# Dynamic convolution and squared-ReLU FFN on one core: convolution steps, closing transposes and group loads moved to other steps of a chunk, the last chunk stored plainly

## Chip, core and metric

The kernel runs on one core of a Trainium2 chip. The metric is the device time of one execution in microseconds; runs of a kernel are summed up by their median. "PE" is TensorE (matrix products; "PEld" its weight loads), "DVE" VectorE, "ACT" ScalarE, "POOL" GpSimd, "SP" SyncE, which here does nothing but issue DMAs, one after another.

## What is computed

First a convolution whose seven weights are made anew for each token and head (a softmax over `weight_gen`), over the seven latest tokens; then an FFN with the square of a ReLU, on 32768 tokens of width 192, hidden width 2048:

```
w   = softmax(weight_gen, axis=-1)                       # 8 x 4096 x 8 heads x 7 taps
out = einsum('bshk,bskhg->bshg', w, the 7 latest x)      # 24 columns per head
h   = out.reshape(32768, 192) @ w_in                     # 192 -> 2048
y   = (maximum(h, 0) ** 2) @ w_out                       # 2048 -> 192
```

## The kernel before, in words

**Chunks and steps.** Token rows are dealt out over 128 partitions, 256 rows each; a chunk is 4 of these rows, 512 tokens, and there are NCH = 64 chunks. A chunk has NJ = 8 steps; a step makes two of the 16 hidden blocks of 128 columns ("fb"). The main loop goes over chunks c = 1 to 63 and in them over steps j = 0 to 7 (written c/j below). All engines work through their instructions in the order in which this loop emits them; the schedule is by hand.

**A step of the main loop** emits, in this order: `mm1(c, j)`, 18 matmuls of 512 columns (line 439), which go in pairs on the upper and the lower 64 rows of the array; `mm2_turned` of two steps earlier (LAG = 2; line 512), 20 such matmuls, which add into four PSUM banks; on ACT two ReLUs (L456) and two squares (L460); on DVE the two `low` parts of the step before (L468), which `mm2_turned` will read a step later; after the last `mm2_turned` of a chunk (at step 1 of the next) `sum_turned`, two ACT copies (L520) and two DVE additions (L522) that free the banks, and a DMA `raw<-raw` (L523); then whatever the dictionary `todo` holds for this step; then `store_turned` in two parts; then on ACT the two `high` parts (L464), from which and from the squares the next step's `low` is made.

**The convolution of chunk m** is a list of 20 steps from `conv_steps`: six of the softmax (0 max, 1 subtract, 2 exp on ACT, 3 sum, 4 reciprocal, 5 multiply; L244 to L249), then thirteen products (L275) and additions (L288), all on DVE over 128x768 elements, then `turn`: a DVE transpose (L402), four DMAs to DRAM (`xd`, L408) and two back (`xT`, L413). Before, `spread` lays these evenly over eight steps from CONV_BEG = 3: (m-2)/3 to (m-1)/2, in numbers 3, 2, 3, 2, 3, 2, 3, 2. At (m-1)/6 three ACT casts (`xh`, L316) and three DVE subtractions (`xl`, L319) split the result, and m/0 reads it.

**Loads and stores.** A group is two chunks. `load_group` issues one DMA of the weights `wt` (L116) and one of `x` (L117), at step 0 of odd chunks, for the group whose convolution begins in the next chunk; it is emitted ahead of everything else of its step. `store_turned(c-1, 0)` at OUT_STEP = 5 is a DVE transpose (L531) and 16 DMAs `o_sb<-raw` (L540); `store_turned(c-1, 1)` at step 6 is a DVE addition that needs `raw<-raw` (L533), a transpose (L534), 8 DMAs and the four of `put_out` to the output (L77). All of them are on SP.

**The last chunk** (63) has its `mm2` the other way round, tokens on the output's partitions (L485, then L774 and L777); its ReLUs, which for odd blocks above 2 are on DVE (L452), also reorder the tokens, so that `put_out` with reads = 1 finds each token by four DMAs, one per 32 partitions. There are three such stores.

Of the kernel before, what the change touches and what calls it, by code (L numbers as in the profile page):

```python
# [21 lines left out]
def kernel(  # L22
# [9 lines left out]
    nc = tc.nc  # L32
# [5 lines left out]
    Q = 32  # L38
    HALO = K - 1
    R = B * S // P  # L40
    PPB = S // R
    TC = 4
    NCH = n_chunks or R // TC
    TG = 8
    CPG = TG // TC
# [4 lines left out]
    NJ = NF // 2  # L50
# [1 line left out]
    WI = ND * P  # L52
    N_PE = 2
    LAG = 2
    CONV_BEG = 3
    OUT_STEP = 5
    NBUF = NF // 2

    const = ctx.enter_context(tc.tile_pool(name="const", bufs=1))
# [12 lines left out]

    def put_out(c, t0, t1, o_sb, reads):
        rows = slice(rows_of(c) + t0, rows_of(c) + t1)
        v = out.rearrange("(q a b r) d -> q b a r d", q=P // Q, a=2 ** reads, r=R)
        for q in range(P // Q):
            nc.sync.dma_start(out=v[q, :, :, rows, :], in_=o_sb[q * Q:(q + 1) * Q, t0:t1])  # L77
# [15 lines left out]
    def rows_of(c):  # L93
        return (c + CPG if c < CPG else c - CPG if c < 2 * CPG else c) * TC
# [8 lines left out]
    def load_group(gi):  # L103
        t0 = rows_of(gi * CPG)
        xt = xin.tile([P, TG + HALO, D], F32, name="xt")
        wt = xin.tile([P, TG, H, K], F32, name="wt")
        x_tiles[gi], w_tiles[gi] = xt, wt
        wf = wt.rearrange("p t h k -> p t (h k)")
        if gi == 0:
            nc.sync.dma_start(out=wf[:, 0:TC, :], in_=wg_v[:, t0:t0 + TC, :])  # L110
            nc.sync.dma_start(out=xt[:, HALO:HALO + TC, :], in_=x_v[:, t0:t0 + TC, :])
            for h in (HALO // 2, 0):
                nc.sync.dma_start(out=xt[:, h:h + HALO // 2, :], in_=x_v[:, t0 - HALO + h:t0 - HALO // 2 + h, :])
            return
        if t0 > 0:
            nc.sync.dma_start(out=wf, in_=wg_v[:, t0:t0 + TG, :])  # L116
            nc.sync.dma_start(out=xt, in_=x_v[:, t0 - HALO:t0 + TG, :])  # L117
            return
        nc.gpsimd.memset(xt[:, 0:HALO, :], 0.0)
        nc.sync.dma_start(out=wf, in_=wg_v[:, 0:TG, :])  # L120
        nc.sync.dma_start(out=xt[:, HALO:, :], in_=x_v[:, 0:TG, :])
        for p0 in range(0, P, PPB):
            nc.sync.dma_start(
                out=xt[p0 + 1:p0 + PPB, 0:HALO, :],
                in_=x_v[p0:p0 + PPB - 1, R - HALO:R, :],
            )
# [97 lines left out]
    def conv_steps(c, on_pe, moving=False):  # L224
# [3 lines left out]
        n = TC * H  # L228
# [28 lines left out]
        prs = {}  # L257
# [139 lines left out]
        def turn():  # L397
            xr = att.tile([P, D // Q, P], F32, name="xr")
            xT = att.tile([P, ND, N], F32, name="xT")
            for k in range(ND):  # L400
                src[k] = xT[:, k]
            nc.vector.transpose(  # L402
                xr.rearrange("p b (t j) -> p t b j", j=Q),
                prs.pop(0).rearrange("p t (b i) -> p t b i", i=Q),
            )
            xd = dram.tile([D, N], F32, name="xd")
            for q in range(P // Q):
                nc.sync.dma_start(  # L408
                    out=xd[:, q * P:(q + 1) * P].rearrange("(b i) n -> i b n", i=Q),
                    in_=xr[q * Q:(q + 1) * Q],  # L410
                )
            for h in range(2):
                nc.sync.dma_start(out=xT[h * D1:(h + 1) * D1], in_=xd.rearrange("(k p) n -> p k n", p=D1))  # L413
# [6 lines left out]
    def mm1(c, j, ops=range(9)):  # L420
        xh, xl = xts[c]["h"], xts[c]["l"]
        if (c, 2 * j) not in phs:
            if c == 0 and j < 2:
                two = [ps_o.tile([P, N], F32, name=f"acc{b + 2 - 2 * j}") for b in range(2)]
            elif c == 0 and j % 2:
                two = [ps_o.tile([P, N], F32, name=f"acc{b}") for b in (2, 3)]
            else:
                two = [ps_h.tile([P, N], F32, name="ph") for _ in range(2)]
            phs[c, 2 * j], phs[c, 2 * j + 1] = two
        two = phs[c, 2 * j], phs[c, 2 * j + 1]  # L430
        seq = [(q, xx, k) for q, xx in ((0, xh), (0, xl), (1, xh)) for k in range(ND)]
        for n, (q, xx, k) in enumerate(seq):
            if n not in ops:
                continue
            for i in range(2):
                rows = slice(i * D1, (i + 1) * D1)
                kw = (k + i) % ND if c < N_PE else k
                w = W[rows, q, j, kw * P:(kw + 1) * P]
                nc.tensor.matmul(two[i], w, two_streams(xx[rows, k]), start=(n == 0), stop=(n == len(seq) - 1))  # L439
# [18 lines left out]
    def square(c, fb):  # L458
        r = rgs[c, fb]
        nc.scalar.activation(r, r, AF.Square)  # L460
# [86 lines left out]
    outs = {}  # L547

    def finish(c, t, to=None):
        if c not in outs:  # L550
            o_sb = op.tile([P, TC, D], F32, name="o_sb", bufs=2)
            outs[c] = o_sb, stage.tile([P, TC, 2 * D], F32, name="raw") if c > 0 else None
        o_sb, tmp = outs[c]
        acc = accs[c][t]
        if c == 0:
            nc.scalar.copy(o_sb[:, 2 * t:2 * t + 2, :], acc[:, 0:2 * D].rearrange("p (t d) -> p t d", t=2))
        else:
            nc.scalar.copy(tmp[:, t, D:], acc[:, D:2 * D])
            to = o_sb[:, t] if to is None else to
            for h, l in ((slice(0, P), slice(2 * P, 2 * D)), (slice(P, D), slice(D, 2 * P))):  # L560
                nc.vector.tensor_tensor(out=to[:, h], in0=acc[:, h], in1=tmp[:, t, l], op=ALU.add)

    def store(c, t0, t1):
        put_out(c, t0, t1, outs[c][0], 1)


    nc.vector.memset(warm, 0.0)
# [115 lines left out]
    def at(c, j, f):  # L683
        todo.setdefault((c + j // NJ, j % NJ), []).append(f)

    def spread(fs, c, j0, j1):
        for i, f in enumerate(fs):
            at(c, j0 + (j1 - j0) * i // len(fs), f)

    def plan_conv(m, a, b):  # L690
        if m == 3:
            for f in a[:2]:
                at(1, 1, f)
            soon[1, 2] = a[2:3]
            spread(a[3:], 1, CONV_BEG, CONV_BEG + NJ)
        elif m > 3:
            spread(a, m - 2, CONV_BEG, CONV_BEG + NJ)
        else:
            for j, fs in enumerate(((), a[4:5], a[5:8], a[8:])):
                for f in fs:  # L700
                    at(1, j, f)
        if m < 2 + CPG:
            soon[m - 1, NJ - 1] = b[0] + b[1][:ND * (m == 2)]
            for f in b[1][ND * (m == 2):]:
                at(m - 1, NJ - 1, f)
        else:
            for f in b:
                at(m - 1, NJ - 2, f)
# [6 lines left out]
    for c in range(1, NCH):  # L715
        tail = c == NCH - 1
        for j in range(NJ):
            if j == 0 and c % 2 and (c + 3) // 2 * CPG < NCH:
                load_group((c + 3) // 2)
            if j == CONV_BEG and 1 < c < NCH - 2:  # L720
                plan_conv(c + 2, *conv_steps(c + 2, 0))
            if c == 1 and j == 0:
                for t in range(TC // 2):
                    finish(0, t)
                store(0, 0, TC)
            mm1(c, j)
            fbs = (2 * j, 2 * j + 1)
            done = None
            if len(pend) == LAG or tail and pend:
                c2, j2 = pend.pop(0)  # L730
                for fb in (2 * j2, 2 * j2 + 1):
                    mm2_turned(c2, fb)
                done = c2 if j2 == NJ - 1 else None
            for f in soon.pop((c, j), []):
                f()
            for fb in fbs:
                relu(c, fb)
            for fb in fbs:
                square(c, fb)
            if not tail:  # L740
                pend.append((c, j))
            for f in late:
                f()
            late.clear()
            if done is not None:
                sum_turned(done)
            for f in todo.pop((c, j), []):
                f()
            if c > 1 and j == OUT_STEP:
                store_turned(c - 1, 0)  # L750
            if c > 1 and j == OUT_STEP + 1:
                store_turned(c - 1, 1)
            if not tail or j < NJ // 2:
                for fb in fbs:
                    high(c, fb)
                    late.append(lambda c=c, fb=fb: low(c, fb))
    c = NCH - 1
# [13 lines left out]
    t, end = TC - 1, range(NF - 4, NF)  # L771
# [6 lines left out]
    o_sb, tmp = outs[c]  # L778
# [33 lines left out]
```

## Time and profile before

| | |
|---|---|
| time, median of 3 runs (lowest to highest) | 2147.02 us (2146.01 to 2150.02) |
| time of the profiled execution | 2143.92 us |
| its span, first to last instruction | 2142.2 us |
| granted TensorE clock, mean | 0.999 (the 2.4 GHz level) |
| busy: PE, PEld, DVE, ACT | 2131.4 (99%), 2044.4 (95%), 1857.5 (87%), 1797.9 (84%) |
| DMA | 195.33 MB, mean 91 GB/s |

The profiled execution is 3.1 us below the median of the timed runs. A share of busy time does not tell whether PE runs at its pace: an instruction that starts late shows as a busy one all the same, so the pace is read from the starts of the matmuls. Times in the rows below count from the start of the span.

### The profile page before, as it was taken

What the parts mean: (1) busy time and instruction counts of PE and PEld (TensorE: products, weight loads), DVE (VectorE), ACT (ScalarE), POOL (GpSimd) and SP (SyncE); (2) the same over time, 40 slices, a digit from 0 to 9 for tenths busy, and PEclk for the clock granted to TensorE, in tenths of its full rate; (3) what the DMA queues carried; (4) which work ended last, traced back from release to release, by engine and by line L of the source; (5) the groups of instructions that cost most, each with busy time, mean ns of one, the idle gap of its engine ahead of it and who ended that gap; (6) DMA issues with size and microseconds to landing.
All of it is one profiled execution on the core that took longest, in us unless ns stands there. A gap on an engine that the chain in (4) does not pass through costs nothing.

```text
span 2142.2 us, 50282 instructions
## 1 busy us (share of the span) xinstructions
PE 2131.4 (99%) x19486; PEld 2044.4 (95%) x19486; DVE 1857.5 (87%) x2866; ACT 1797.9 (84%) x3492; POOL 9.9 (0%) x18
## 2 busy tenths in 40 slices
PE   9999999999999999999999999999999999999998
PEld 9889999999999999999999999999999999999998
DVE  9988988888889888888898888888988888889884
ACT  8888888888888888888888888888888888888886
POOL 0000000000000000000000000000000000000000
PEclk9999999999999999999999999999999999999999
DMA  8433334333233332333433333334333233333231
GB/s 230 100 80 102 88 66 104 88 96 92 62 105 93 91 105 62 93 102 84 103 89 66 104 87 97 91 63 104 91 93 104 62 92 94 91 104 87 67 76 39
DMA packets 324303, 195.33 MB, mean 91 GB/s; under 512 B 225128, under 2 KB 282472, under 8 KB 320224
## 3 DMA queue, kind: packets, MB, share of 16 engines
q1 hardware_dynamic: 322768, 188.58, 34.9%
q0 software_dynamic: 1296, 3.54, 0.9%
q8 instruction: 152, 2.49, 0.5%
q14 instruction: 87, 0.71, 0.1%
HBM read 106.39 MB, written 49.55 MB: 73 GB/s over the span
## 4 chain that ended last, share of the span: by engine, by line
PE 96%; DVE 1%; SPq 1%; ACT 1%; DMA 0%; issue 0%; DVEq 0%; ACTq 0%
PE acc L512 49%; PE ph L439 45%; PE acc L476 1%; PE acc L485 1%; SPq L540 1%; DMA xT<-xd 0%; DVE gl L468 0%; ACT gh L464 0%; ACT rg L460 0%; DMA out_dram<-o_sb 0%; ACT rg L456 0%; DVE du L184 0%; DVE du L186 0%; PE acc L439 0%; DVE xl L319 0%
## 5 line engine op out<-in xcount | busy, mean ns | idle before, releaser
L512 PE MATMUL acc<-gh,V 64*128 64x512 f32 x5952 | 1085.2, 377 | 0.0
L512 PE MATMUL acc<-gl,V 64*128 64x512 f32 x3968 | 917.4, 378 | 0.6 <-DVE gl L468 0.5
L439 PE MATMUL ph<-xh,W 64*128 64x512 f32 x6084 | 917.7, 376 | 0.2
L512 PEld LDWEIGHTS acc<-gh,V 64*128 64x128 f32 x5952 | 779.9, 186 | 25.6
L468 DVE TENSOR_TENSOR gl<-rg,gh 128x512 fp32r<-128x512 f32 x1008 | 641.3, 675 | 119.6 <-ACT gh L464 119.6
L439 PEld LDWEIGHTS ph<-xh,W 64*128 64x128 f32 x6084 | 709.8, 186 | 24.8 <-issue 0.7
L456 ACT ACTIVATE rg<-ph 128x512 f32<-128x512 f32 x992 | 537.8, 594 | 218.1 <-PE ph L439 217.4
L460 ACT ACTIVATE rg<-rg 128x512 f32<-128x512 f32 x1008 | 579.8, 631 | 0.2
L512 PEld LDWEIGHTS acc<-gl,V 64*128 64x128 f32 x3968 | 556.3, 186 | 23.6 <-DVE gl L468 3.3
L464 ACT CAST gh<-rg 128x512 fp32r<-128x512 f32 x1008 | 574.2, 624 | 3.2 <-PE acc L485 3.2
L439 PE MATMUL ph<-xl,W 64*128 64x512 f32 x3042 | 459.3, 376 | 0.0
L275 DVE TENSOR_TENSOR pr<-xt,wt 128x768 f32<-128x768 f32 (+1 forms) x441 | 411.1, 945 | 2.3
L439 PEld LDWEIGHTS ph<-xl,W 64*128 64x128 f32 x3042 | 355.3, 186 | 11.6
L288 DVE TENSOR_TENSOR pr<-pr 128x768 f32<-128x768 f32 x366 | 345.8, 945 | 0.1
L319 DVE TENSOR_TENSOR xl<-xT,xh 128x512 fp32r<-128x512 f32 x186 | 117.5, 687 | 123.0 <-ACT xh L316 120.2
L316 ACT CAST xh<-xT 128x512 fp32r<-128x512 f32 x186 | 102.6, 622 | 1.8 <-DMA xT<-xd 1.7
L246 ACT ACTIVATE wt<-wt 128x224 f32<-128x224 f32 x62 | 24.2, 391 | 94.8 <-DVE wt L245 94.8
L522 DVE TENSOR_TENSOR raw<-acc,raw 128x512 f32<-128x512 f32 x124 | 79.0, 675 | 3.8 <-ACT raw L520 3.8
L520 ACT COPY raw<-acc 128x512 f32<-128x512 f32 x124 | 66.5, 596 | 0.0
L402 DVE STREAM_TRANSPOSE xr<-pr 128x768 f32<-128x768 f32 x62 | 60.7, 978 | 2.1
L534 DVE STREAM_TRANSPOSE raw<-raw 64x512 f32<-64x512 f32 x62 | 43.6, 704 | 2.1
L531 DVE STREAM_TRANSPOSE raw<-raw 128x512 f32<-128x512 f32 x62 | 43.7, 704 | 0.0
(93 smaller groups left out, 450.4 us busy)
## 6 DMA issues: line engine op xcount, KB each, us to landing
xT<-xd SPq DMA_DIRECT2D x124, 384.0 KB
xt<-in_x_dram SPq DMA_DIRECT2D x30, 1344.0 KB
out_dram<-o_sb SPq DMA_DIRECT2D x252, 96.0 KB
xd<-xr SPq DMA_DIRECT2D x248, 96.0 KB
o_sb<-raw SPq DMA_DIRECT2D x1488, 16.0 KB
raw<-raw SPq DMA_DIRECT2D x62, 128.0 KB
wt<-in_weight_gen_dram SPq DMA_DIRECT2D x31, 224.0 KB
raw<-in_moe_w_in_dram SPq DMA_DIRECT2D x16, 192.0 KB
```

Source lines behind the costliest of these rows:

```text
L275: tt(out=dst, in0=src, in1=wf[:, t0 * H:t1 * H, k:k + 1].broadcast_to([P, m, G]), op=ALU.mult)
L288: tt(out=prs[k0], in0=prs[k0], in1=prs.pop(k), op=ALU.add)
L316: nc.scalar.copy(parts["h"][:, k, n], src[k][:, n])
L319: tt(out=parts["l"][:, k, n], in0=src[k][:, n], in1=parts["h"][:, k, n].bitcast(F32), op=ALU.subtract)
L439: nc.tensor.matmul(two[i], w, two_streams(xx[rows, k]), start=(n == 0), stop=(n == len(seq) - 1))
L456: nc.scalar.activation(r, ph, AF.Relu)
L460: nc.scalar.activation(r, r, AF.Square)
L464: nc.scalar.copy(gh, rgs[c, fb])
L468: nc.vector.tensor_tensor(out=gl, in0=rgs.pop((c, fb)), in1=ghs[c, fb].bitcast(F32), op=ALU.subtract)
L512: nc.tensor.matmul(accs[c][b + h], w, two_streams(g[rows]), **fl)
L520: nc.scalar.copy(X[:, k], acc[b])
L522: nc.vector.tensor_tensor(out=X[:, k], in0=acc[b + 1], in1=X[:, k], op=ALU.add)
```

## The change

- The 20 convolution steps of a chunk (from chunk 4 on) begin at step 1 instead of 3 and are dealt out in the numbers 2, 1, 4, 1, 3, 0, 3, 3, 0, 3 over ten steps, (m-2)/1 to (m-1)/2. Chunk 3's keep their steps.
- `store_turned` moves from steps 5 and 6 to steps 3 and 4.
- `load_group` moves from step 0 to step 5 of the odd chunks (not in chunk 1).
- The last chunk's `turn` makes four transposes of 128x192 instead of one of 128x768, and writes them in an order such that the tokens come out plainly; its three stores are one DMA each instead of four.

```diff
-    CONV_BEG = 3
-    OUT_STEP = 5
+    CONV_BEG = 1
+    CONV_SLOTS = (2, 1, 4, 1, 3, 0, 3, 3, 0, 3)
+    OUT_STEP = 3
+    LOAD_STEP = 5
...
         rows = slice(rows_of(c) + t0, rows_of(c) + t1)
+        if reads == 0:
+            nc.sync.dma_start(out=out.rearrange("(p r) d -> p r d", r=R)[:, rows, :], in_=o_sb[:, t0:t1])
+            return
...
-            nc.vector.transpose(
-                xr.rearrange("p b (t j) -> p t b j", j=Q),
-                prs.pop(0).rearrange("p t (b i) -> p t b i", i=Q),
-            )
+            pr = prs.pop(0).rearrange("p t (b i) -> p t b i", i=Q)
+            if c < NCH - 1:
+                nc.vector.transpose(xr.rearrange("p b (t j) -> p t b j", j=Q), pr)
+            else:
+                for t in range(TC):
+                    nc.vector.transpose(xr[:, :, t * Q:(t + 1) * Q].rearrange("p b (i m) -> p b m i", i=2), pr[:, t])
...
     def store(c, t0, t1):
-        put_out(c, t0, t1, outs[c][0], 1)
+        put_out(c, t0, t1, outs[c][0], 1 if c == 0 else 0)
...
-            spread(a[3:], 1, CONV_BEG, CONV_BEG + NJ)
+            spread(a[3:], 1, 3, 3 + NJ)
         elif m > 3:
-            spread(a, m - 2, CONV_BEG, CONV_BEG + NJ)
+            fs = iter(a)
+            for j, n in enumerate(CONV_SLOTS):
+                for _ in range(n):
+                    at(m - 2, CONV_BEG + j, next(fs))
...
-            if j == 0 and c % 2 and (c + 3) // 2 * CPG < NCH:
+            if j == (LOAD_STEP if c > 1 else 0) and c % 2 and (c + 3) // 2 * CPG < NCH:
                 load_group((c + 3) // 2)
             if j == CONV_BEG and 1 < c < NCH - 2:
                 plan_conv(c + 2, *conv_steps(c + 2, 0))
```

## Rows read from the trace of the kernel before

**Rows 1.** The page: the chain that ended last, share of the span by engine.
```profile
PE 96%; DVE 1%; SPq 1%; ACT 1%; DMA 0%; issue 0%; DVEq 0%; ACTq 0%
```
**Rows 2.** Timeline of PE, first matmuls of steps 30/0, 30/1, 31/0: start, length, instruction, count.
```profile
1006.07 0.95 PE L439 MATMUL ph<-xh,W 64*128 64x512 f32 x6
...
1010.31 0.81 PE L439 MATMUL ph<-xh,W 64*128 64x512 f32 x6
...
1039.02 0.94 PE L439 MATMUL ph<-xh,W 64*128 64x512 f32 x6
```
**Rows 3.** Timeline of PE: first matmuls of step 4/0 and of step 63/0.
```profile
149.20 0.38 PE L439 MATMUL ph<-xh,W 64*128 64x512 f32 x2
...
2094.51 0.38 PE L439 MATMUL ph<-xh,W 64*128 64x512 f32 x1
```
**Rows 4.** Timeline of all engines, step 30/0, where its second product begins.
```profile
1007.57 1.24 DVE L468 TENSOR_TENSOR gl<-rg,gh 128x512 fp32r<-128x512 f32 x2
...
1008.02 0.51 PE L512 MATMUL acc<-gh,V 64*128 64x512 f32 x2
...
1008.27 0.48 PE L512 MATMUL acc<-gl,V 64*128 64x512 f32 x2
```
**Rows 5.** Timeline of DVE, steps 29/6 to 30/3; the bracket is idle time and its end.
```profile
1002.67 1.90 DVE L319 TENSOR_TENSOR xl<-xT,xh 128x512 fp32r<-128x512 f32 x3 [2.00 <-ACT xh L316]
1004.48 0.95 DVE L275 TENSOR_TENSOR pr<-xt,wt 128x768 f32<-128x768 f32 x1
...
1006.22 0.68 DVE L533 TENSOR_TENSOR raw<-raw 64x512 f32<-64x512 f32 x1
...
1014.29 1.28 DVE L468 TENSOR_TENSOR gl<-rg,gh 128x512 fp32r<-128x512 f32 x2
1015.49 1.27 DVE L522 TENSOR_TENSOR raw<-acc,raw 128x512 f32<-128x512 f32 x2
...
1021.47 0.98 DVE L402 STREAM_TRANSPOSE xr<-pr 128x768 f32<-128x768 f32 x1
...
1023.55 0.38 DVE L244 TENSOR_REDUCE mx<-wt 128x32 f32<-128x224 f32 x1
```
**Rows 6.** Timeline of ACT, the copies of `sum_turned` at step 30/1.
```profile
1014.46 1.07 ACT L520 COPY raw<-acc 128x512 f32<-128x512 f32 x2
```
**Rows 7.** Timeline of SP's DMA issues, from step 30/4 to 31/3.
```profile
1022.48 2.65 SPq L408 DMA_DIRECT2D xd<-xr  x4
1026.83 1.32 SPq L413 DMA_DIRECT2D xT<-xd  x2
1032.46 16.42 SPq L540 DMA_DIRECT2D o_sb<-raw  x24
1048.99 3.06 SPq L77 DMA_DIRECT2D out_dram<-o_sb  x4
1052.10 0.43 SPq L116 DMA_DIRECT2D wt<-in_weight_gen_dram  x1
```
**Rows 8.** Stretches of a group's load: length, busy time by engine, clock, DMA share, GB/s.
```profile
1052.10:1053.10 1.00, 1.00 (x12) 1.00 (x10) 1.00 (x3) 0.55 (x2) 0.00 (x0) 1.00 0.38 147
1053.10:1054.60 1.50, 1.50 (x17) 1.50 (x15) 1.47 (x3) 1.00 (x3) 0.00 (x0) 1.00 0.98 270
...
1052.10:1058.30 6.20, 6.20 (x61) 6.20 (x59) 5.17 (x10) 3.63 (x9) 0.00 (x0) 1.00 0.87 298
```
**Rows 9.** Tile `wt`, window 1040 to 1090: first and last start of its first reader.
```profile
L244 DVE TENSOR_REDUCE mx<-wt x2: 377/378/378, 1056.5 to 1089.4; 128x32 f32<-128x224 f32 x2
```
**Rows 10.** The last chunk: DVE and SP timelines, and the chain's last piece of `mm1`.
```profile
2111.08 0.69 DVE L452 TENSOR_SCALAR rg<-ph 128x512 f32<-128x512 f32 x1
...
2110.90 4.15 PE ph L439 x36
...
2133.69 0.36 DVE L780 TENSOR_TENSOR o_sb<-ph,raw 128x192 f32<-128x192 f32 x1
...
2128.66 10.99 SPq L77 DMA_DIRECT2D out_dram<-o_sb  x16
```

## The prediction

> **What bounds the kernel now.** I read the chain first: 96% of it is PE [rows 1], so nothing counts that does not delay PE or stand at the two ends. Next PE's pace, from the starts of its matmuls. From step 30/1 to 31/0 seven steps take 1039.02 - 1010.31 = 28.71 us, 4.10 each, but step 30/0 takes 1010.31 - 1006.07 = 4.24 [rows 2]: 0.14 too long, though PE shows as busy throughout. It is no single case: from 4/0 to 63/0 59 chunks take 2094.51 - 149.20 = 1945.3 us, 32.97 each [rows 3], and eight steps at 28.71 / 7 are 32.81. So 0.16 us a chunk, 59 x 0.16 = **9.4 us**, is lost to this wait and a few larger ones.
>
> What does PE wait for in step 30/0? Its second product should start some 0.22 after the first (step 4.10 over 19 pairs), at 1008.24; it starts at 1008.27, with 0.48 for the pair [rows 4], and from there on the two halves of each pair, which had run 0.14 apart, run together (six matmuls take 0.81 in 30/1 and 0.95 in 30/0 [rows 2]): the first half has slipped by that much. It reads the first `gl` of step 29/6, which DVE only begins at 1007.57 and makes in about 0.64. DVE is late because of what 29/6 put ahead of it: three `xl` that had to wait 2.00 us for ACT, then a product, an addition and the second part of `store_turned`, from 1004.48 to 1007.57 [rows 4, 5]. So the loss is DVE's queue at step 6, not DVE's total.
>
> There is a second thing to see: at step 1 `sum_turned` starts on DVE at 1015.49, right behind two `gl` (1014.29) [rows 5], although ACT's first copy is done by about 1015.0 [rows 6]. It ends at 1016.76, and PE wants the banks again at step 2. This is as tight as the other.
>
> **The change part by part.**
>
> *Convolution steps and OUT_STEP.* Nothing is added on DVE; the same work goes to other steps. Prices, start to start [rows 4, 5]: product or addition 0.87 (two from 1004.48 to 1006.22); two `gl` 1.20; three `xl` 1.81; second part of the store 1.35 (1006.22 to 1007.57); the `turn` 0.91 and the store's first transpose 0.65 (both taken just under the duration of such a row); two sums 1.20; small softmax steps 0.4 to 0.6 (`mx` 0.38). DVE per step, `gl` included:
> before, steps 0 to 7: 2.9, 5.0, 3.0, 2.0, 2.2, 4.0, 6.1, 3.8;
> after: 3.8, 3.2, 3.9, 4.1, 3.4, 3.8, 3.0, 3.8.
> Before, step 6 is 2.0 over PE's 4.10 and step 1 0.9; after, no step is over. Now the queue after the change, in chunk 30's times. At 29/6 the `xl` still end at 1004.48, as ACT sets them. The `gl` of 29/6 come directly behind: first one by 1005.1, wanted at 1008.1, so 3.0 early instead of 0.1 late. Three products (2.61) and the next `gl`: 1008.9 against 1012.2, 3.3 early. Three more: 1012.7 against 1016.3, 3.6. `sum_turned` then finds DVE free and follows ACT's copies, 1015.0 to 1016.2, 0.5 sooner than now. Two softmax steps, `gl` at 1017.6 (wanted 1020.4, 2.8 early: the least). Two additions and the `turn` end at 1020.9 (now 1021.47 + 0.91 = 1022.4), `gl` at 1021.5 (3 early), four softmax and product steps and the transpose, `gl` at 1025.6 (3), a product and 1.35, `gl` at 1029.1 (3.7). DVE never owes PE anything; 2.8 us is the cover, and if it goes each us more costs PE one. So all of the 9.4 us should go. ACT's load stays; `exp` moves to step 2, after its input. Ends: 8.0 (59 x 0.137, the larger waits stay) to 9.6.
>
> *SP's queue.* It now reaches `xd` at 1020.9. Rows 7 give 2.65 for its issues, 1.70 until it has landed, 1.32 for `xT`: 1026.6. Y is ready (1025), so 24 `o_sb` in 16.5 and four stores in 3.1 follow without a gap: 1046.2. `xT` is read at about 1034.8 and lands some 4 after issue: early by 4. SP is free for the next chunk's `raw<-raw` at about 1049.
>
> *Loads.* Now they are issued at 1052.10, ahead of the odd chunk's own work, and first read at 1089.4: 37 us ahead [rows 7, 9]. After, they stand behind the odd chunk's stores, at 1046.2 in these times, and the first reader comes at 1016.2 + 32.8 = 1049.0: **2.8 us ahead**. How long does `wt` take? By 1054.60, 2.5 after issue, 147 + 405 = 552 KB had moved [rows 8], more than `wt` (224) and what could be left of three stores (288). Lower end 1.6 (0.43 issue and 224 KB at 298 GB/s), upper end 6.2, if it landed only with all of the group. I take 2.5, the nearest row: just in time. At 6.2 DVE would stand 3.4, of which 2.8 is covered: 0.6 for PE, 29 times, 17 us. `x` lands by 1052.4, its first product comes at 1056. The Trainium skill, DMA: Bandwidth & Descriptors, section Rules for kernel authors, says to issue a DMA early, compute, and wait on it late; this part does the contrary, and by that rule the load becomes a rival (below). No run shows yet which.
>
> *The last chunk.* Its `turn` is four transposes instead of one: 0.98 now; four between 4 x 0.25 (a quarter of the row) and 4 x 0.7. Chunk 62 has no convolution beside it (nothing of a chunk 64), so DVE covers up to 2.8 more; I take 0. Store: the result is ready at 2133.69 + 0.36 = 2134.05, but SP is then in a row of 16 issues from 2128.66 to 2139.65 [rows 10], and the span ends 2.5 after it, at 2142.2. After, SP has chunk 62's stores behind it earlier and only three issues: last one 2134.1 to 2134.7 (10.99 / 16 = 0.69; 0.43 for 128 rows of `wt`), and the end at 2137.2: **5.0 saved**. Ends: 3.5 (a DMA of 128 rows takes as long to land as four) to 5.3. Against it: the store's two parts now precede the DVE ReLU of step 63/5, 2.0 us in all, some of it in idle time; that ReLU ends at about 2113.3 instead of 2111.8, and PE, which does the last 36 matmuls from 2110.90, wants its bank at about 2112.9 [rows 10]. **0.4 lost** (0 to 0.8).
>
> *Start.* Chunk 0 to 2/0 keep their order: nothing.
>
> **Sum.** 9.4 + 5.0 - 0.4 = 14.0 us. The profiled execution would go from 2143.92 to 2129.9. The median of the runs stands 3.1 above it (2147.02); kept, that gives **2133.0 us**.
>
> **The rivals.**
>
> A. *The wait only moves.* PE's matmuls run in pairs; a pair's second half starts 0.14 after its first in some stretches and together with it in others (0.95 for six against 0.81 [rows 2]), so one half can slip without the other, and freeing one wait may uncover another at step 2, as the banks come free late. For it: both waits are as tight. Against it: DVE is 2.8 early everywhere, `sum_turned` by 0.5. Then only the end gains: 2147.0 - 4.6 = 2142.4. Chance 0.10, half of it beyond the bound below.
>
> B. *The load comes late* (slower). The trace gives `wt` 2.8 us and it needs 2.5; DVE covers another 2.8. Beyond 3.1 late PE stands, in each of 29 groups, and the gain is gone at 14.0 / 29 = 0.5 more, so at 6.1 us after issue, or an issue that late. SP has no gap ahead of it, so each stretched issue adds. With 1 us of PE per group: 2133 + 29 = 2162. For it: `xd` and `xT` wait on landings in front of it. Against it: nothing else moves on the queues then. Chance 0.10, a third of it within the bound or faster.
>
> C. *The end gives less*, as the 128-row store lands late or the ReLUs of chunk 63 hold PE longer: 2135 to 2137. Chance 0.08. The forecast itself (2129 to 2136): 0.72.
>
> **How the numbers follow.** A measurement of this kernel can tell about 0.2% (4.3 us) from no change, so the bound is 2142.7. Faster: 0.72 + 0.08 + 0.05 + 0.01 = 0.86; within: 0.05 + 0.02 = 0.07; slower 0.07. The range: the forecast's terms at their ends (8.0 + 3.5 - 0.8 = 10.7 to 9.6 + 5.3 = 14.9) give 2132.1 to 2136.3; timed runs differ by 4 us, and what keeps them above the profiled one may be waits of the same kind, which 2.8 us of cover would also take: down to 2129. Upwards it takes in A, to 2143; of B's end only the part up to there, as the rows put `wt` at 2.5.
>
> **What would show it.** In the profile after: step 30/0 as long as the others, eight steps in 32.81; `gl` of step 6 done 3 us ahead of its product; DVE's first addition of `sum_turned` right after ACT's first copy; `xd` issued some 1.6 earlier in a chunk; SP without a gap from `xT` to the last store; `mx` of an even chunk with an idle time before it that ends with `wt`, or none; three store issues at the end, the last at about 2.5 us before the end of the span. It would be wrong if a step other than 0 is longer than 4.10, or if `mx` of even chunks waits over 2.8 us for `wt`.

## The result and the profile after

The changed kernel takes 2129.07 us in the median (2128.74 to 2129.46), beside 2147.49 (2146.01 to 2150.02) of the kernel before: a ratio of 0.9916, 95% interval 0.9904 to 0.9929, so 18.4 us less. 14.0 were forecast (2133.0 us). The profiled execution went from a span of 2142.2 us to 2126.9, 15.3 less. Line numbers of the changed kernel are 5 to 10 higher: `mm1` is L446, `mm2_turned` L519, `low` L475, `put_out` L78 (plain) and L82.

The chain that ended last, share by engine [rows 1]:

```profile
PE 99%; ACT 0%; POOL 0%; issue 0%; DVE 0%; POOLq 0%
```

PE's timeline: the first matmuls of steps 30/0, 30/1 and 31/0 [rows 2], then those of 4/0 and 63/0 [rows 3] (start, length, instruction, count):

```profile
1001.50 0.81 PE L446 MATMUL ph<-xh,W 64*128 64x512 f32 x6
...
1005.60 0.81 PE L446 MATMUL ph<-xh,W 64*128 64x512 f32 x6
...
1034.31 0.81 PE L446 MATMUL ph<-xh,W 64*128 64x512 f32 x6
```
```profile
148.53 0.38 PE L446 MATMUL ph<-xh,W 64*128 64x512 f32 x2
...
2084.12 0.59 PE L446 MATMUL ph<-xh,W 64*128 64x512 f32 x4
```

Step 30/0 now takes 4.10 like the seven behind it. From 4/0 to 63/0 the 59 chunks take 1935.6 us, 32.81 each, where they took 32.97: 9.7 us less, and nothing is left of the wait (no step of these chunks is longer than 4.10). Six matmuls take 0.81 in all three rows: both halves of a pair now run together through the chunk.

DVE's timeline, steps 29/6 to 30/3 [rows 5] (the bracket is idle time and what ended it):

```profile
998.10 1.90 DVE L324 TENSOR_TENSOR xl<-xT,xh 128x512 fp32r<-128x512 f32 x3 [1.97 <-ACT xh L321]
999.91 1.29 DVE L475 TENSOR_TENSOR gl<-rg,gh 128x512 fp32r<-128x512 f32 x2
...
1010.37 1.29 DVE L529 TENSOR_TENSOR raw<-acc,raw 128x512 f32<-128x512 f32 x2 [1.55 <-ACT raw L527]
1011.87 0.39 DVE L249 TENSOR_REDUCE mx<-wt 128x32 f32<-128x224 f32 x1 [0.21 <-DMA wt<-in_weight_gen_dram]
...
1012.60 1.28 DVE L475 TENSOR_TENSOR gl<-rg,gh 128x512 fp32r<-128x512 f32 x2
...
1015.78 0.98 DVE L409 STREAM_TRANSPOSE xr<-pr 128x768 f32<-128x768 f32 x1
```

The `gl` follow the `xl` at once; `sum_turned` waits for ACT's copy instead of coming late; and `mx` has a short wait for the load. SP's timeline over the same stretch [rows 7], with the stores and the group's load of the odd chunk 29 at its head:

```profile
1006.02 3.08 SPq L82 DMA_DIRECT2D out_dram<-o_sb  x4
1009.15 0.44 SPq L121 DMA_DIRECT2D wt<-in_weight_gen_dram  x1
...
1016.79 2.38 SPq L415 DMA_DIRECT2D xd<-xr  x4
1020.91 1.32 SPq L420 DMA_DIRECT2D xT<-xd  x2
1022.32 17.27 SPq L547 DMA_DIRECT2D o_sb<-raw  x24
1039.70 3.09 SPq L82 DMA_DIRECT2D out_dram<-o_sb  x4
```

The load goes out at 1009.15 and `mx` runs at 1011.87, 2.7 us later, where it had 37 us before [rows 7, 9]. Over the whole run the table of waits has it as

```profile
DVE mx L249 <- DMA wt<-in_weight_gen_dram: 5.6, 10, 2.0
```

that is 10 waits with 5.6 us in all, the longest (2.0) at the start of the program. The end, from the timelines of DVE and SP and from the chain [rows 10]:

```profile
2102.05 1.45 DVE L459 TENSOR_SCALAR rg<-ph 128x512 f32<-128x512 f32 x2
...
2100.52 4.43 PE ph L446 x36
...
2123.58 0.36 DVE L790 TENSOR_TENSOR o_sb<-ph,raw 128x192 f32<-128x192 f32 x1
...
2115.16 3.06 SPq L82 DMA_DIRECT2D out_dram<-o_sb  x4
2121.93 2.37 SPq L78 DMA_DIRECT2D out_dram<-o_sb  x3
```

The first line is the two DVE ReLUs of step 63/5, now behind the store's two parts. SP is idle when the last three stores come; from the last result (2123.94) to the end of the span it is 3.0 us, where it was 8.1. The last 36 matmuls of `mm1` take 4.43 instead of 4.15.

### The profile page after: what moved, and what is told of

Its sections match the earlier page's. It is cut to its first block, busy times and chain, and to the rows that moved or that the text cites. A ratio compares the mean times of both kernels' runs of the same rounds, so it can differ in the third digit from the quotient of the medians.

```text
span 2126.9 us, 50423 instructions
## 1 busy us (share of the span) xinstructions
PE 2121.8 (100%) x19486; PEld 1865.2 (88%) x19486; DVE 1864.2 (88%) x2869; ACT 1797.9 (85%) x3492; POOL 9.9 (0%) x18
## 4 chain that ended last, share of the span: by engine, by line
PE 99%; ACT 0%; POOL 0%; issue 0%; DVE 0%; POOLq 0%
PE acc L519 50%; PE ph L446 46%; PE acc L483 1%; PE acc L492 1%; PE acc L446 0%; PE acc L355 0%; PE acc L581 0%; ACT rg L467 0%; ACT gh L471 0%; PE ph L343 0%; ACT rg L461 0%; PE ph L787 0%; PE acc L343 0%; PE acc L784 0%; DVE o_sb L790 0%
## 5 line engine op out<-in xcount | busy, mean ns | idle before, releaser
L519 PE MATMUL acc<-gh,V 64*128 64x512 f32 x5952 | 976.9, 376 | 0.0
L446 PE MATMUL ph<-xh,W 64*128 64x512 f32 x6084 | 822.4, 376 | 0.3 <-ACT rg L461 0.3
L519 PE MATMUL acc<-gl,V 64*128 64x512 f32 x3968 | 752.7, 376 | 0.0
L475 DVE TENSOR_TENSOR gl<-rg,gh 128x512 fp32r<-128x512 f32 x1008 | 641.2, 675 | 12.8 <-ACT gh L471 12.8
L446 PEld LDWEIGHTS ph<-xh,W 64*128 64x128 f32 x6084 | 576.1, 186 | 82.3 <-issue 0.7
L519 PEld LDWEIGHTS acc<-gh,V 64*128 64x128 f32 x5952 | 563.5, 186 | 78.8
L519 PEld LDWEIGHTS acc<-gl,V 64*128 64x128 f32 x3968 | 375.6, 186 | 53.1 <-DVE gl L475 0.6
L280 DVE TENSOR_TENSOR pr<-xt,wt 128x768 f32<-128x768 f32 (+1 forms) x441 | 416.6, 946 | 2.2
L446 PE MATMUL ph<-xl,W 64*128 64x512 f32 x3042 | 411.4, 376 | 0.0
L446 PEld LDWEIGHTS ph<-xl,W 64*128 64x128 f32 x3042 | 288.3, 186 | 40.1
L540 DVE TENSOR_TENSOR raw<-raw 64x512 f32<-64x512 f32 x62 | 41.8, 675 | 0.0
```

The source lines that it names most:

```text
L280: tt(out=dst, in0=src, in1=wf[:, t0 * H:t1 * H, k:k + 1].broadcast_to([P, m, G]), op=ALU.mult)
L475: nc.vector.tensor_tensor(out=gl, in0=rgs.pop((c, fb)), in1=ghs[c, fb].bitcast(F32), op=ALU.subtract)
L519: nc.tensor.matmul(accs[c][b + h], w, two_streams(g[rows]), **fl)
```

## The experiments

Each kernel was timed beside the kernel before on the same chip. That one scatters much more than the changed kernel: from 2143.4 to 2149.7 us in the 18 runs beside e1 to e4.

### The parts alone: e1 to e4

Four kernels, each the kernel before with one part of the change.

e1, the store's steps:
```diff
-    OUT_STEP = 5
+    OUT_STEP = 3
```

> The kernel before with OUT_STEP = 3 alone (store_turned at steps 3 and 4). Queue theory (DVE's queue at step 6 is what PE waits for): the second store part, 1.35 us, no longer stands ahead of the gl of step 6; the first of these is ready 1.3 us ahead of PE instead of 0.1 behind, so steps 0 become 4.10 and the 9.4 us go: about 2138 us. The end of the span stays as before, since the 16 store issues stay; chunk 63 loses some 0.3. Rival A (a freed wait only moves, as the two halves of a pair slip in turn): some other step becomes 0.14 longer in each chunk and the time stays at 2147. If the 3.6 us by which the timed runs of before stand above its profiled one come from DVE's missing cover, they go too: 2135.

Measured: 2134.37 us (2133.93 to 2134.39) beside 2146.42, ratio 0.994 (0.9925 to 0.9955): 12 us less, as in the variant expected in which the surplus of the timed runs goes too. All steps from 4/0 on are 4.10.

e2, the convolution's steps:
```diff
-            spread(a, m - 2, CONV_BEG, CONV_BEG + NJ)
+            fs = iter(a)
+            for j, n in enumerate(CONV_SLOTS):
+                for _ in range(n):
+                    at(m - 2, CONV_BEG + j, next(fs))
```
with CONV_BEG and CONV_SLOTS as in the change, and chunk 3's steps kept.

> The kernel before with the convolution steps alone dealt out anew (from step 1, in the numbers 2 1 4 1 3 0 3 3 0 3). Queue theory: a product and an addition, 1.74 us, no longer stand ahead of the gl of step 6, which come 1.6 us ahead of PE: 9.4 us go, 2138 us (2135 if the surplus of the timed runs comes from missing cover). Rival A: 2147, with another step 0.14 longer.

Measured: 2134.14 us (2133.69 to 2134.60), ratio 0.994 (0.9923 to 0.9957), again 12 us less, and again no step 0 is longer than the rest. DVE's timeline at 29/6, of e2 (the product and the addition are gone, the store's second part is still there):

```profile
997.94 1.90 DVE L320 TENSOR_TENSOR xl<-xT,xh 128x512 fp32r<-128x512 f32 x3 [2.50 <-ACT xh L317]
999.75 0.68 DVE L534 TENSOR_TENSOR raw<-raw 64x512 f32<-64x512 f32 x1
1000.46 0.70 DVE L535 STREAM_TRANSPOSE raw<-raw 64x512 f32<-64x512 f32 x1
1001.10 1.24 DVE L469 TENSOR_TENSOR gl<-rg,gh 128x512 fp32r<-128x512 f32 x2
```

So either move does: 1.35 or 1.74 us less in front of these `gl` are each enough for a lateness of 0.1. The two parts of the change do the same work twice; what the changed kernel gains beyond either, some 5 us, is the end (e4). Rival A (the wait moves) is out in both: no other step grew.

e3, the load:
```diff
-            if j == 0 and c % 2 and (c + 3) // 2 * CPG < NCH:
+            if j == (LOAD_STEP if c > 1 else 0) and c % 2 and (c + 3) // 2 * CPG < NCH:
```
with LOAD_STEP = 5.

> The kernel before with load_group alone moved from step 0 to step 5 of odd chunks. DVE's queue is as before, so the 0.14 us at step 0 stay in every chunk. If the larger waits, and the surplus of the timed runs over the profiled one, come from the group's load running beside the xd and xT transfers of odd chunks, they go: ACT no longer waits for xT, and the time falls by 1.6 to 4 us, to 2143 to 2146, with less scatter. If they come from DVE's missing cover alone: 2147, with the scatter of before.

Measured: 2141.87 us (2141.57 to 2142.21), ratio 0.9978 (0.9968 to 0.9988): 4.6 us less, somewhat more than the 1.6 to 4 expected, and a scatter of 0.6 us in nine runs instead of 6.3. The 0.14 at step 0 is there in all 59 chunks, and there is no larger wait.

e4, the last chunk: the four transposes, and `put_out` with reads = 0.
```diff
-        put_out(c, t0, t1, outs[c][0], 1)
+        put_out(c, t0, t1, outs[c][0], 1 if c == 0 else 0)
```

> The kernel before with the last chunk's part alone (four transposes, three plain stores). SP theory of the end: the last issue goes out at about 2134.2 instead of 2139.1 in the times of before's span, and the span ends 2.5 to 3 us later: 5.1 us less, 2142.4 us, all steps 0 still 4.24. If a DMA of 128 rows lands as late as four of 32: 3.5 less, 2144.

Measured: 2143.12 us (2140.43 to 2146.13), ratio 0.9984 (0.9974 to 0.9993): 3.3 us less, with an interval of 1.5 to 5.6 because the scatter stays. The trace is sharper: from the first matmul of the last `mm2` to the end of the span it takes 22.0 us, as in the changed kernel, where before it took 27.2: 5.15 less.

Why does the load alone stop the scatter? The profiled execution of e4 has seven steps longer than 4.30 from chunk 4 on, all of them step 0 of an even chunk (that of before has five, also steps 0 of even chunks), and the table of waits has seven waits of ACT for `xT`: one in chunk 1, as every execution has, and six ahead of six of these seven steps. In e3 there is only the one in chunk 1 (e4, then e3):

```profile
ACT xh L319 <- DMA xT<-xd: 4.1, 7, 1.6
```
```profile
ACT xh L317 <- DMA xT<-xd: 0.9, 1, 0.9
```

The worst of them, in e4's timelines of SP, ACT, DVE and PE (37/3 to 38/1):

```profile
1250.32 0.43 SPq L119 DMA_DIRECT2D wt<-in_weight_gen_dram  x1
1250.80 0.42 SPq L120 DMA_DIRECT2D xt<-in_x_dram  x1
...
1252.82 3.18 SPq L413 DMA_DIRECT2D xd<-xr  x4
1260.99 1.32 SPq L418 DMA_DIRECT2D xT<-xd  x2
...
1267.02 1.66 ACT L319 CAST xh<-xT 128x512 fp32r<-128x512 f32 x3 [1.60 <-DMA xT<-xd]
...
1267.67 1.90 DVE L322 TENSOR_TENSOR xl<-xT,xh 128x512 fp32r<-128x512 f32 x3 [3.71 <-ACT xh L319]
...
1269.37 0.94 PE L444 MATMUL ph<-xh,W 64*128 64x512 f32 x6
...
1275.31 0.81 PE L444 MATMUL ph<-xh,W 64*128 64x512 f32 x6
```

The group's load is issued at 1250.32, 2.5 us ahead of `xd`. While its 1568 KB move, `xd` lands late, and `xT`, which has to wait for it, goes out late: 5.0 us from the last `xd` issue to `xT`'s, where it was 1.7 in a chunk without a load [rows 7]. It is so throughout: in the odd chunks 3 to 59 this distance is 3.9 us in the median in before (2.9 to 4.9) and 3.8 in e4, but 1.7 in e1, e3 and the changed kernel; in the even chunks it is 1.7 in all of them. ACT then waits 1.60 for `xT`, DVE 3.71 for ACT where it waited 2.00 at 29/6 [rows 5], the `gl` come that much later, and step 38/0 takes 5.94 instead of 4.24. That `xT` is late by another amount in each execution, and that this is the scatter of the kernel before, follows from e3, where both go together; one execution of each kernel was profiled, so it was not seen from one execution to the next. The profiled execution of before had little of these waits. In e3 the load is behind `xT` in SP's order and can no longer delay it. In e2 it still stands 1.9 us ahead of `xd` and holds `xT` up (the distance is 4.8 us in the median of the odd chunks, and ACT waits twice from chunk 4 on, 0.27 and 0.72 us), but DVE has the time and PE sees nothing of it. In e1 it is out of the way by itself, since the store's DMAs ahead of it are done sooner; SP's timeline there:

```profile
1044.07 0.43 SPq L116 DMA_DIRECT2D wt<-in_weight_gen_dram  x1
...
1050.77 1.82 SPq L408 DMA_DIRECT2D xd<-xr  x4
1054.30 1.33 SPq L413 DMA_DIRECT2D xT<-xd  x2
```

The load is 6.7 us ahead of `xd`, and `xT` goes out 1.7 after the last `xd`. So each of the three moves alone ends the larger waits, in a way of its own: the convolution's by DVE's time, the store's by SP's queue (and DVE's time), the load's by its order.

### How much cover DVE has: e5, e6 and e12

Two or four useless DVE reductions at step 1, put into the changed kernel:

```diff
+            if 3 < c < NCH - 1 and j == 1:
+                for _ in range(2):
+                    nc.vector.tensor_reduce(out=scr, in_=W[:, 0, 0:2, :].bitcast(F32), axis=AX.X, op=ALU.max)
```

> The changed kernel with two useless DVE reductions over 128x768 at step 1 of chunks 4 to 62, behind the softmax steps and ahead of the gl of step 1. From a product's 0.87 us (same size) they take some 1.7 us. Cover theory: in the changed kernel's trace the first gl of 30/1 is done at 1013.24 and PE's second product of 30/3 wants it at about 15.96, so DVE has 2.7 us to give: no cost, 2129 us, every step 4.10. If the cover is smaller than the trace says, up to 59 x 1.7 = 100 us.

> As with two, but four reductions, some 3.5 us. Cover theory: 0.8 us more than DVE has at this place, PE stands 0.8 in each of 59 chunks (step 3 of a chunk, for gl of step 1): +47 us, 2176 us. Rival (what counts is DVE's idle time of a whole chunk, 32.8 - 28.9 = 3.9 us): 3.5 still fits, 2129 us.

Measured: 2165.53 us with two (2162.9 to 2167.3), 2328.66 with four (2327.3 to 2336.9). Neither expectation held. The timeline of DVE in e5 shows what had been left out:

```profile
1025.26 1.29 DVE L530 TENSOR_TENSOR raw<-acc,raw 128x512 f32<-128x512 f32 x2 [1.55 <-ACT raw L528]
1029.70 0.39 DVE L250 TENSOR_REDUCE mx<-wt 128x32 f32<-128x224 f32 x1 [3.15 <-DMA wt<-in_weight_gen_dram]
1030.12 0.39 DVE L251 TENSOR_TENSOR wt<-wt,mx 128x224 f32<-128x224 f32 x1
1030.43 1.93 DVE L762 TENSOR_REDUCE scr<-W 128x2 f32<-128x768 f32 x2
1032.28 1.28 DVE L476 TENSOR_TENSOR gl<-rg,gh 128x512 fp32r<-128x512 f32 x2
```

The reductions delay the `turn`, so `xd`, so everything behind it on SP, and the load is last in that row (e12 tests this): `mx` of even chunks waits 2.1 us in the mean

```profile
DVE mx L250 <- DMA wt<-in_weight_gen_dram: 61.8, 29, 3.1
```

and the cover of 2.7 us has to pay for both, 1.85 and 2.1: 1.2 short, in 29 even chunks 36 us, which is what was measured (36.5 more than the changed kernel's 2129.07). In the profiled execution it is 38.4, of which 37.1 at step 3 of even chunks and 1.3 at the step behind it. With four, odd chunks lose 28.9 us, 0.96 each, beside 0.8 expected; even chunks wait 3.3 for `wt` besides and lose 6 each. Part of that is PE's clock (last section).

e12 is e5 with the load back at step 0:

```diff
-    LOAD_STEP = 5
+    LOAD_STEP = 0
```

> The kernel of e5 (two useless reductions at step 1 of each chunk) with the group's load back at step 0, as in e9. In e5 only even chunks lost time, and there mx waited 2.1 us for wt, since everything on SP, the load too, came some 1.8 later. If the cover of 2.7 us was right and was spent twice in e5 (reductions and the wait for wt), this one has only the 1.75 us of the reductions to cover: no wait of mx for wt, no loss, 2128.7 us. If the cover is simply smaller than 2.7, the 36 us stay: 2165.

Measured: 2128.79 us (2128.60 to 2129.12), no step longer than 4.10 from chunk 4 on, and of `mx` only the program's first wait is left:

```profile
DVE mx L250 <- DMA wt<-in_weight_gen_dram: 2.0, 1, 2.0
```

The same 1.85 us of work in every chunk cost nothing once the load stands elsewhere, so in e5 it was the load's new place that used up the cover. e12 by itself shows only that the cover is no less than 1.85; its size comes from e6's odd chunks, which have no load to wait for: the four reductions took 3.8 us there and PE lost 0.96, which leaves 2.9, beside 2.7 expected and 2.8 in the prediction. These chunks also show that DVE's idle time of the whole chunk (3.9 us) is not the measure, since 3.8 us of work at one step did not fit.

### How late the load may be: e7 and e8

The changed kernel with four useless DMAs ahead of each group's load, in e8 eight:

```diff
+                if c > 1:
+                    for e in range(4):
+                        q, d0 = e % 4, e // 4 * Q
+                        nc.sync.dma_start(out=scr[q * Q:(q + 1) * Q, :, d0:d0 + Q], in_=ident[0:Q].rearrange("p (t i) -> p t i", t=TC))
                 load_group((c + 3) // 2)
```

> The changed kernel with four useless DMAs of 16 KB (128 pieces of 128 bytes, to DRAM) on SP ahead of each group's load: the load goes out some 2.6 us later, and DVE's first softmax step of even chunks waits for wt some 2.7 us instead of 0.2. Cover theory (rival B with its place): the wait is as long as DVE's cover, so PE loses next to nothing, 2129 to 2134 us, while the waits of mx for wt grow from 5.6 to about 75 us in sum. If every wait for wt reached PE: 2129 + 29 x 2.5 = 2200.

> As with four, but eight such DMAs: the load goes out some 5.2 us later, mx waits about 5.3 us, of which 2.7 are covered: PE stands 2.6 us in each of 29 even chunks, +75 us, 2200 us. If the cover were DVE's whole idle time, 1.4 x 29 = 41: 2170. If SP's queue catches up on the way, less than half of it.

Measured: 2136.13 us (2134.65 to 2136.56) with four, 2223.25 (2218.6 to 2226.7) with eight. The waits for `wt`, e7 and then e8:

```profile
DVE mx L250 <- DMA wt<-in_weight_gen_dram: 81.6, 30, 3.5
```
```profile
DVE mx L250 <- DMA wt<-in_weight_gen_dram: 164.2, 30, 7.4
```

With four the waits sum to 81.6 us, 2.7 for each of 29 groups, and PE loses 7, where 0 to 5 were expected; with eight they sum to 164, 5.6 a group, and PE loses 94, 3.2 a group, where 2.6 were expected (2.9 by the wait that came; the last section has where some of the rest went). So rival B has its place and about its price: the first 2.7 us of a wait cost next to nothing, the rest is PE's. In the changed kernel a group waits 0.1 us in the mean and 1.1 at most (behind the program's first), so it stands some 2.5 us from that edge, and 1.6 at the worst.

### Is the load's move needed? e9, e10, e11

e9 is the changed kernel with LOAD_STEP = 0, e10 the changed kernel once more on the same chip, e11 has LOAD_STEP = 3 (on SP ahead of the 24 `o_sb` instead of behind the stores) and chunk 63's store at steps 5 and 6.

```diff
-    LOAD_STEP = 5
+    LOAD_STEP = 3
...
-            if c > 1 and j == OUT_STEP:
+            o = OUT_STEP + (2 if tail else 0)
+            if c > 1 and j == o:
                 store_turned(c - 1, 0)
-            if c > 1 and j == OUT_STEP + 1:
+            if c > 1 and j == o + 1:
```

> The changed kernel with the group's load back at step 0 of odd chunks, all else as changed. With DVE's cover a late xT no longer reaches PE: 2129 us, and small scatter, although ACT waits for xT in some odd chunks and no mx waits for wt. If moving the load is what removes the larger waits in the changed kernel too, they come back: 2131 to 2134 us, with a scatter of some us.

> The changed kernel itself, beside the others on the same chip: 2129.1 us, 0.7 us of scatter.

> The changed kernel with the load at step 3 (on SP ahead of the 16 o_sb DMAs instead of behind the stores) and chunk 63's store at steps 5 and 6 as before. The load is then issued some 19 us sooner and no mx waits for wt; the DVE ReLU of step 63/5 is no longer behind the store: 0.3 us less, 2128.8 us, hardly to be told from the changed kernel. If the load now delays the o_sb DMAs behind it so that the store's end is late: the same or more.

Measured, all beside 2144.38 of the kernel before: e9 2128.69 us (2128.50 to 2128.96), e10 2128.91 (2128.74 to 2131.26), e11 2128.37 (2128.31 to 2128.37). The load's move brings nothing beside the other two. It was expected that ACT would wait for `xT` again in e9 and DVE's cover hide it, but there was nothing to hide: with the store at step 3 the load goes out 6.4 us ahead of `xd` there, much as in e1, and ACT's one wait for `xT` is that of chunk 1:

```profile
ACT xh L321 <- DMA xT<-xd: 0.7, 1, 0.7
```

One run of e10 was 2.5 us longer: its trace has chunk 1 begin that much later, behind waits of ACT and DVE for the first loads of `x`, and everything after it is the same. In e11 the last 36 matmuls of `mm1` take 4.15 again, as before the change, and no `mx` waits but the program's first. e11 is at least as fast as the changed kernel, and its `mx` has no wait that could grow to the edge of e7.

## Why the prediction was right, and where it was off

- **The wait at step 0** and its cause: right. The 0.137 us is gone in all 59 chunks (8.1 us), in e1 and e2 with either half of the reordering, and the `gl` stand in the trace of after where the sum by steps put them: the `xl` ended at 999.91, exactly chunk 30's predicted 1004.48 less the 4.57 us by which that chunk began earlier; the load went out at 1009.15, predicted 1008.8; the `turn` ended 0.4 later than predicted.
- **The larger waits** were mis-sized: this is the term that was off. They were taken from one profiled execution, 9.4 less 8.1, some 1.3 us, and given to DVE's queue at large. e3 and e4 show their source, the load beside `xd` and `xT`, and another size: 4.6 us in the median of the timed runs (e3, 2.6 to 6.9 by its interval). That is about the 1.3 us of the profiled execution and the 3.1 us by which the median stood above it, so these 3.1 were mostly such waits. The prediction kept them as a fixed addition. Its terms at their ends gave no less than 2132.1; it named their going only as something that may be, for the low end of the range, 2129, and 2129.07 came out. That the time lies within the range is thus owed to this remark and not to the sum, and in part to luck. The reason given there, that DVE's cover would take these waits too, is not what acted either: e2 shows that the cover would do it, but in the changed kernel `xT` is no longer late (1.7 us behind `xd`, as in any even chunk). With the profiled execution alone the sum holds better: 15.3 measured, 14.0 forecast.
- **The load**: 2.8 us ahead of its reader was forecast, 2.7 measured; `wt` lands in about that time (2.5 taken), so that `mx` waits now and then. (The lower end, 1.6, was added up wrongly: 0.43 and 224 KB at 298 GB/s are 1.2. Nothing rested on it.) That DVE's cover hides it was right, and e6, e7, e8 and e12 measured both the cover and what lies beyond it. But the sum had not seen that the old place cost anything: its SP part followed the load only forward, not the `xd` and `xT` that were queued behind it.
- **The end**: 5.0 forecast, 5.15 measured, and 0.28 lost in chunk 63's `mm1` (0.4 forecast). e11 takes the 0.28 back.
- **The start** was taken at nothing, and nothing there was changed. It differs from execution to execution: step 1/3 begins at 62.83 before, 62.16 after and 64.58 in e10. 0.7 of the 15.3 us is of this kind and not of the change.

So 15.3 = 9.7 (59 chunks) + 4.9 (end, less 0.28) + 0.7 (start). The 18.4 of the medians leave 3.8 us beside the 9.7 and the 4.9; by e3 they are larger waits of the timed runs, but no trace of those runs shows it.

## What to carry to other kernels

Where PE shows as busy throughout, look for steps that are longer than their neighbours; the queue of the engine that feeds that step, written out instruction by instruction with the trace's durations, gave the size of the fault and of the cure to a few tenths of a us. The scatter of the timed runs is a term of the sum too: ask what in the kernel can vary, and look at every transfer that is queued behind a large load, before taking the distance between median and profile as fixed. Slack on an engine is one account from which all late arrivals are paid; a load moved to just ahead of its reader draws on the same account as the work that the reorder made room for.

## What the runs showed of the hardware

A PE that stood still for some us came back at the lower of its two clock levels. In e6 PE waits 4.83 us for `gl` in 30/3; the stretches of 4 us around it (length, busy time of PE, PEld, DVE, ACT, POOL, then granted clock, DMA share, GB/s):

```profile
1031.00:1035.00 4.00, 0.06 (x2) 0.00 (x0) 3.88 (x5) 3.56 (x8) 0.00 (x0) 0.86 0.66 268
1035.00:1039.00 4.00, 3.11 (x14) 2.50 (x16) 3.93 (x6) 0.90 (x2) 0.00 (x0) 0.50 0.00 2
1039.00:1043.00 4.00, 4.00 (x32) 3.30 (x30) 3.86 (x9) 0.55 (x2) 0.00 (x0) 0.78 0.49 98
1043.00:1047.00 4.00, 4.00 (x42) 3.45 (x38) 3.96 (x7) 3.05 (x7) 0.00 (x0) 1.00 0.70 162
```

The wait ends at 1035.89. The granted clock is 0.50 (1.2 GHz) right after it and 1.00 (2.4 GHz) again by 1043, and six matmuls of 0.81 take 1.23 at 1039.89. In e6 such a stretch comes with each of the 28 waits of 2.9 us and more, in e8 with 9 of its 29 waits (all of them 1.3 to 4.4 us). PE's waits for `gl` in e6 and in e8:

```profile
PE acc L520 <- DVE gl L476: 137.3, 59, 6.3
```
```profile
PE acc L520 <- DVE gl L476: 75.4, 29, 4.4
```

From 4/0 to 63/0 these executions took 208 and 98 us more than the changed kernel, so they lost more than the waits alone; the mean clock of the run is 0.972 in e6 and 0.993 in e8, where it was 1.000. A wait that goes beyond the cover can therefore be dearer than its length.
